# Splitting the first K tile's load of a decode-attention kernel into 16 and 112 partitions

## The chip, the cores and the metric

The kernel runs on one core of one Trainium2 chip. The metric is the device time of one execution in microseconds; the time of a kernel is the median of its runs.

## The reference

One decode step: grouped-query attention with 16 query heads on 8 KV heads over a cache of 65536 positions with 256 elements each, and a small gated feed-forward part, mixed by a sigmoid gate. Everything is bf16.

```python
q = (x @ wq)                                     # x: 1 x 448, wq: 448 x 4096 -> 16 heads x 256
scores = einsum("bhqd,bhkd->bhqk", q, k) * (256 ** -0.5)   # k, v: 8 heads x 65536 x 256, repeated twice
p = softmax(scores, axis=-1)
a = einsum("bhqk,bhkd->bhqd", p, v).reshape(1, 1, 4096) @ wo   # wo: 4096 x 448
gate, up = x @ W_gate, x @ W_up                  # 448 x 1792 each
b = (gate * (gate > 0) * up) @ W_down            # 1792 x 448
g = sigmoid((x * gate_w).sum(-1))
out = g * a + (1 - g) * b
```

K and V are 268 MB each, so nearly all bytes that the kernel reads are the two caches.

## The kernel before

**Tiles.** The K cache is read in 32 tiles, four for each of the 8 KV heads (`NTH = 4`, `NT = 32`). A tile is 16384 positions: 128 partitions with 128 positions each, 64 KB for a partition, 8 MB in all. `k_src(n)` gives the source of tile `n`, in which the 128 partitions' pieces follow one another in the cache. The V cache has 32 tiles of the same size. Three buffers of that size, `ring[0]` to `ring[2]`, hold what is on chip: K tiles go to 1 and 2 in turn, V tiles to 0 (the last head's V tiles to 1 and 2 as well). At the start, `ring[0]` holds the weights: wq (L626, and its last 64 rows L627), W_down (L675), then W_gate and W_up (L640, L642). At the end, wo is loaded in six pieces (L785).

**Order of transfers.** All large loads are issued from SP's program, in the order of the list `order`: K tile 0, wq, K tile 1, W_down, K tile 2, W_gate and W_up, then K and V tiles in turn. Each entry has a planned time `t`, which is only a key to sort by. `dma(engine, key, semaphore, function, dependences)` adds a transfer; `op` adds an instruction. `finish` sorts each engine's program by key. A transfer adds 16 to its semaphore when it has landed, and `finish` counts these, so that a dependence on a transfer becomes a wait for that count. `emit` writes out a program and puts the waits in front of each instruction; a wait for a count that the engine has already waited for is left out. `free(("k", n))` gives the work after which a buffer may be filled again; for K tiles 0 and 1 there is none. The two small loads, x and gate_w, are issued from ACT (L421, L422).

**What is done with a K tile.** DVE transposes it in place in four parts (L529, the operations `tr`), TensorE multiplies it with the query (L540, two halves `qk[n, 0]` and `qk[n, 1]`), DVE takes the maximum (L703) and ACT the exponential (L705). K tile 2 can be issued only when `qk[0, 1]` has read the buffer. For head 0 the query must be there first: TensorE projects it from wq (L501), ACT copies it (L630), DVE transposes it and spreads it into `xm` (L632, L513), ACT copies `xcur` (L634). DVE works through its program in order, and the four transposes of tile 0 stand ahead of L632. V tiles are multiplied by the probabilities on TensorE (L584) after a copy on ACT (L591).

**The start of SP's program.** The first operation of SP's program is written out ahead of the block in which the other engines' programs stand, and the rest in SP's part of the block, with one memory of the waits (`seen_sp`):

```python
        seen_sp = {}
        pl.emit("sp", progs["sp"][:1], nc.sync, seen_sp)
        with nc.Block() as block:
            @block.sync
            def _(e):
                pl.emit("sp", progs["sp"][1:], e, seen_sp)
```

Of the kernel before, what the change touches and what calls it, by code (L numbers as in the profile page):

```python
# [27 lines left out]
class _Plan:  # L28
# [8 lines left out]
    def op(self, eng, key, fn, deps=(), tag=None):  # L37
        eng, cls = {"pv": ("pe", "pv"), "dx": ("dv", "dx"), "ap": ("ac", "ap")}.get(eng, (eng, eng))
        o = _Op(eng, key, fn, deps, tag=tag, cls=cls)
        self.ops.append(o)  # L40
        return o

    def dma(self, eng, key, sem, fn, deps=()):
        if sem not in self.dsem:
            self.dsem[sem] = self.es.enter_context(self.nc.semaphore("d_" + sem))
        o = _Op(eng, key, fn, deps, dma=sem)
        self.ops.append(o)
        return o
# [212 lines left out]
def bass_gated_mix__gqa_block_cached__glu_gated_reglu__decode_kernel(  # L261
# [35 lines left out]
    with es:  # L297
# [3 lines left out]
        ring = [sb("ring%d" % i, [128, U * DH], BF) for i in range(NRING)]  # L301
# [68 lines left out]
        pl = _Plan(nc, es)  # L370
        op, dma = pl.op, pl.dma
# [23 lines left out]
        t = 3.0  # L395
# [10 lines left out]
        def place(kind, i):  # L406
            if kind == "k":
                return 1 + i % 2
            if kind == "v":
                return 1 + i % 2 if i >= NT - NTH else 0  # L410
            return {"vp": 2, "wo": 0}[kind]

        for kind, i, _ in order:
            if kind in ("k", "v") or (kind, i) in (("wo", 0), ("vp", 0)):
                r = place(kind, i)
# [101 lines left out]
        def k_src(n):  # L517
            h, t_ = divmod(n, NTH)
            return A_k_cache[0, h, t_ * TK:(t_ + 1) * TK, :].rearrange("(p u) d -> p (u d)", u=U)
# [7 lines left out]
        def f_trans(sl, w):  # L527
            v = ring[sl][:, w * 8192:(w + 1) * 8192].bitcast(U32)
            return lambda e: e.transpose(v, v)  # L529
# [34 lines left out]
        def free(key):  # L564
            out_ = []
            for f in freed[key]:
                out_.append(l_[f] if isinstance(f, str) else qk[f[1], 1] if f[0] == "k" else pv[f[1]])
            return out_
# [55 lines left out]
        for kind, i, t in sorted(issue, key=lambda q: q[0] != "wq"):  # L624
# [51 lines left out]
            elif kind == "k":  # L676
                n = i
                h, t_ = divmod(n, NTH)
                sl = slot["k", n]
                kd = dma("sp", t, "r%d" % sl, lambda e, n=n, sl=sl: e.dma_start(ring[sl][:], k_src(n)), free(("k", n)))  # L680
                tk = max(tL["k", n], last.get("free", 0))
                tr = [op("dv", tk + 4.5 * w, f_trans(sl, w), [kd]) for w in range(4)]
                if n > 1:
                    tr[1].deps.append(aexp[n - 2])
                if t_ == 0:
# [82 lines left out]
            elif kind in ("v", "vp"):  # L768
                if kind == "v":
                    n, lo, hi = i, 0, U  # L770
                    sl = slot["v", n]
                    dep = dma("sp", t, "r%d" % sl, lambda e, sl=sl, n=n: e.dma_start(ring[sl][:], v_src(n)), free(("v", n)))
                else:
                    n, (lo, hi) = NT - 1, PIECES[i]
                    sl = slot["vp", 0]
# [7 lines left out]
            elif kind == "wo":  # L783
                lo, hi = WO[i]
# [19 lines left out]
        progs = pl.finish()  # L804

        seen_sp = {}
        pl.emit("sp", progs["sp"][:1], nc.sync, seen_sp)
        with nc.Block() as block:

            @block.sync  # L810
            def _(e):
                pl.emit("sp", progs["sp"][1:], e, seen_sp)

            @block.tensor
            def _(e):
                prog = progs["pe"]
                at = lambda o: prog.index(o)
                seen = {}
                k0 = [at(pv[NTH * (h - 1)] if h else qk[0, 0]) for h in range(H)]
                km = [at(pv[NTH * (h - 1) + 2] if h else qk[2, 0]) for h in range(H)]  # L820
                kc = [at(last["h3", h]) for h in range(H)]
                t0, t1, t2 = at(pv[NT - NTH]), at(pv[NT - 2]), at(pv[NT - 1]) + 1
                pl.emit("pe", prog[:k0[0]], e, seen)
                inner, outer = {}, {}
                for h in range(H):
                    inner[h, 0], inner[h, 1] = prog[k0[h]:km[h]], prog[km[h]:kc[h]]
                    outer[(h,)] = prog[kc[h]:k0[h + 1] if h < H - 1 else t0]
                pl.emit_nest("pe", e, inner, outer, seen, {("pv", a, 0) for a in range(2)} )
                pl.emit_loop("pe", e, {(0,): prog[t0:t1], (1,): prog[t1:t2]}, seen)
                pl.emit("pe", prog[t2:], e, seen)  # L830

            @block.vector
            def _(e):
                pl.emit_heads("dv", progs["dv"], e, [first["dv", h] for h in range(1, H)] + [last["ocp", H - 1]], 1)

            @block.scalar
            def _(e):
                pl.emit_heads("ac", progs["ac"], e, [first["ac", h] for h in range(1, H)] + [pc[NT - NTH]], 1)

            @block.gpsimd  # L840
            def _(e):
                pl.emit("gp", progs["gp"], e)
# [33 lines left out]
```

## Time and profile before

| | before |
|---|---|
| time, median of 3 runs | 1275.85 us (1275.74 to 1276.02) |
| profiled execution: span from first to last instruction | 1274.3 us |
| bytes read | 549.03 MB, 431 GB/s over the span |
| busy share: PE, DVE, ACT, POOL | 29%, 49%, 6%, 0% |
| issue of K tile 0 on SP | at 0.72 us |
| first transpose of K tile 0 on DVE | at 22.81 us |
| first matmul of the q projection | at 31.49 us |
| issue of K tile 2 on SP | at 50.70 us |
| output's transfer issued | at 1273.11 us |

The profile shows one execution. Its own whole time is not listed apart from its span; the runs' median is 1.55 us above the span, which stands for what lies ahead of the first and behind the last instruction. In the lines of the profile, PE is TensorE's matmul, PEld its weight load, DVE VectorE, ACT ScalarE, POOL GpSimd, and an engine's name with a q is its queue of instructions that issue transfers. `L529` is line 529 of the kernel.

### The profile page before, as it was taken

The numbers are of one execution on the slowest core, as the hardware profiler recorded it, in microseconds if no ns is written. First come the engines' busy times: TensorE is split into PE (matmuls) and PEld (weight loads), VectorE is DVE, ScalarE is ACT, GpSimd is POOL, SyncE is SP. The second block draws the span as 40 slices with busy tenths as digits, with TensorE's granted clock in tenths as the row PEclk, the third lists the DMA queues.
The fourth block names the chain that finished last, engine by engine and source line by source line (L and its number), as shares of the span: only waits on it lengthen the run. The fifth ranks groups of instructions, "written<-read, shape, count | busy, mean of one in ns | idle before, by whom it ended". The sixth has DMA issues, their size and how long they took to land.

```text
span 1274.3 us, 10240 instructions
## 1 busy us (share of the span) xinstructions
PE 365.9 (29%) x4497; PEld 151.4 (12%) x4505; DVE 630.1 (49%) x309; ACT 78.0 (6%) x163; POOL 4.6 (0%) x23
## 2 busy tenths in 40 slices
PE   0534321133320332312233222323302332112525
PEld 0101110011110111101111110111100111001201
DVE  4777655553455633557433565335654355553300
ACT  0001100010000100001000010000000010000100
POOL 1000000000000000000000000000000000000000
PEclk9766665666655666656666656666566666566667
DMA  9999999999999999999999999999999999999998
GB/s 411 430 436 432 426 430 434 432 443 432 430 432 432 434 442 430 430 434 430 438 438 430 430 434 430 440 438 428 430 434 430 444 434 428 430 436 430 442 421 369
DMA packets 11389, 549.13 MB, mean 431 GB/s; under 512 B 1267, under 2 KB 1654, under 8 KB 2294
## 3 DMA queue, kind: packets, MB, share of 16 engines
q1 hardware_dynamic: 11378, 549.03, 99.7%
q8 instruction: 4, 0.07, 0.0%
q14 instruction: 3, 0.02, 0.0%
q10 hardware_dynamic: 4, 0.00, 0.0%
HBM read 549.03 MB, written 0.00 MB: 431 GB/s over the span
## 4 chain that ended last, share of the span: by engine, by line
DMA 81%; PE 16%; DVE 2%; ACT 1%; issue 1%; SPq 0%; ACTq 0%
DMA ring<-in_A_v_cache_dram 74%; PE O L584 13%; DMA ring<-in_A_wo_dram 3%; DMA ring<-in_A_wq_dram 2%; DMA ring<-in_A_k_cache_dram 2%; DVE ring L529 1%; PE ST L540 1%; ACT pcur L591 1%; PE O L501 1%; PE A_ps L551 0%; SPq L785 0%; SPq L776 0%; PE O L653 0%; DVE ring L660 0%; PE A_ps L653 0%
## 5 line engine op out<-in xcount | busy, mean ns | idle before, releaser
L529 DVE STREAM_TRANSPOSE ring<-ring 128x4096 uint32<-128x4096 uint32 x128 | 557.6, 4413 | 196.9 <-DMA ring<-in_A_k_cache_dram 196.9
L584 PE MATMUL O<-ring,pcur 128*4 128x512 bf16 x2048 | 187.3, 545 | 790.4 <-ACT pcur L591 781.9
L703 DVE TENSOR_REDUCE nmb<-ST 128x1 f32<-128x512 f32 x32 | 22.1, 692 | 345.9 <-PE ST L540 345.9
L584 PEld LDWEIGHTS O<-ring,pcur 128*4 128x4 bf16 x2048 | 59.3, 111 | 914.8 <-ACT pcur L591 794.6
L540 PE MATMUL ST<-ring,xcur 128*16 128x512 bf16 x2048 | 136.7, 420 | 44.3 <-DVE ring L529 43.7
L540 PEld LDWEIGHTS ST<-ring,xcur 128*16 128x16 bf16 x2048 | 62.4, 92 | 112.1 <-DVE ring L529 48.6
L705 ACT ACTIVATE P_sb<-ST,nmb 128x512 bf16<-128x512 f32 x32 | 44.6, 1392 | 368.3 <-DVE nmb L703 368.3
L591 ACT COPY pcur<-ptp 128x256 bf16<-128x256 bf16 x32 | 13.2, 415 | 732.6 <-DMA ring<-in_A_v_cache_dram 732.6
L607 DVE TENSOR_SCALAR o_sb<-O,rcm 128x256 bf16<-128x256 f32 x8 | 3.8, 479 | 61.1 <-PE O L584 61.1
L730 DVE TENSOR_TENSOR P_sb<-P_sb,hs 128x1024 bf16<-128x1024 bf16 x16 | 18.9, 1222 | 8.1 <-ACT hs L724 8.1
L735 PE MATMUL PT<-identb,P_sb 128*128 128x128 bf16 x128 | 14.5, 282 | 17.6 <-DVE P_sb L730 17.3
L501 PE MATMUL O<-ring,P_sb 128*128 128x512 bf16 x28 | 8.5, 477 | 17.3 <-DMA ring<-in_A_wq_dram 17.3
L735 PEld LDWEIGHTS PT<-identb,P_sb 128*128 128x128 bf16 x128 | 10.7, 127 | 19.9 <-DVE P_sb L730 19.9
L744 ACT COPY ptp<-PT 128x256 bf16<-128x256 bf16 x32 | 10.3, 375 | 23.0 <-PE PT L735 23.0
L705 ACT ACTIVATION_READ_ACCUMULATOR P_sb<-ST,nmb 128x1 f32 x32 | 8.3, 258 | 0.0
L501 PEld LDWEIGHTS O<-ring,P_sb 128*128 128x128 bf16 x28 | 3.2, 117 | 22.2 <-issue 20.5
L551 PE MATMUL A_ps<-ring,attnA 128*1 128x224 bf16 x64 | 5.3, 322 | 1.1 <-DMA ring<-in_A_wo_dram 1.0
L719 PE MATMUL M_ps<-identf,hs 128*2 128x128 f32 x8 | 2.3, 283 | 10.0 <-DVE hs L717 10.0
L756 DVE RECIPROCAL rc<-M_ps 128x2 f32<-128x2 f32 x8 | 1.4, 171 | 7.5 <-PE M_ps L755 7.5
L755 PE MATMUL M_ps<-hs,ones_f 128*128 128x2 f32 x16 | 4.5, 352 | 0.0
L722 PE MATMUL M_ps<-mx,nselT 2*128 2x1 f32 x16 | 3.2, 268 | 3.0 <-DVE mx L721 3.0
L755 PEld LDWEIGHTS M_ps<-hs,ones_f 128*128 128x128 f32 x16 | 4.0, 311 | 0.0
(93 smaller groups left out, 68.6 us busy)
## 6 DMA issues: line engine op xcount, KB each, us to landing
ring<-in_A_v_cache_dram SPq DMA_DIRECT2D x1, 4096.0 KB, 22.1
ring<-in_A_wq_dram SPq DMA_DIRECT2D x1, 3072.0 KB, 28.9
ring<-in_A_v_cache_dram SPq DMA_DIRECT2D x1, 3072.0 KB, 28.8
ring<-in_B_W_down_dram SPq DMA_DIRECT2D x1, 1568.0 KB, 53.0
ring<-in_B_W_gate_dram SPq DMA_DIRECT2D x1, 1344.0 KB, 26.3
ring<-in_B_W_up_dram SPq DMA_DIRECT2D x1, 1344.0 KB, 29.2
ring<-in_A_wo_dram SPq DMA_DIRECT2D x1, 1232.0 KB, 33.0
ring<-in_A_v_cache_dram SPq DMA_DIRECT2D x1, 1024.0 KB, 30.7
```

Source lines behind the costliest of these rows:

```text
L501: ins = e.matmul(QN_ps, xw3[:, kt, 31 - m:159 - m], rhs, start=(kt == 0 and m == 0), stop=(kt == R3 and m == J // 4 - 1))
L529: return lambda e: e.transpose(v, v)
L540: ins = e.matmul(bank[32 * w:32 * w + 16, :], xcur[:, x0:x0 + 16], ktv[sl][:, u0:u0 + 16, c, :, r_], start=(b == 0 and c == 0 and r_ == 0) ...
L551: ins = e.matmul(A_ps[32 * g:32 * g + 1, 0:D2], lhsT, rhs[:, g * D2:(g + 1) * D2], start=start, stop=stop, skip_group_check=True, tile_pos ...
L584: ins = e.matmul(OP[32 * g:32 * g + 4, :], pcur[a % 2][:, 4 * k:4 * k + 4], ring[sl][:, k * 512:(k + 1) * 512], start=False, stop=False, s ...
L591: pc[n] = op("ap", max(tp - 5, last["tev", h] - 0.5), lambda e: e.copy(pcur[a % 2][:].rearrange("p (k i) -> p k i", i=4), ptp[:].rearrange ...
L703: smax[n] = op("dv", sx, lambda e, n=n, t_=t_: e.tensor_reduce(NM[:, t_:t_ + 1], ST[n % 2][:], AX.X, ALU.max, negate=True), [qk[n, 1], las ...
L705: aexp[n] = op("ac", sx + 1, lambda e, n=n, t_=t_: e.activation(P_sb[:, t_:2048:4], ST[n % 2][:], ACTF.Exp, bias=NM[:, t_:t_ + 1], scale=1 ...
L730: rsc = op("dv", tt, lambda e, pb=pb: e.tensor_tensor(pb, pb, X[:, 12:16].unsqueeze(1).to_broadcast([128, 256, 4]), ALU.mult), [h7, aexp[n]])
L735: ins = e.transpose(PT[rd][:, s * 128:(s + 1) * 128], P_sb[:, (rd * 8 + s) * 128:(rd * 8 + s + 1) * 128], identb[:, :])
L744: ins = e.copy(dst, src)
L755: l3 = mop("pe", T + 19, lambda e: e.matmul(LS_ps, ones_f[:, :], X[:, 6:8], start=True, stop=True), [l2, c_one], tag="l3")
```

## The change

K tile 0 is loaded by two transfers in place of one. The first takes partitions 0 to 15, that is 16 pieces of 64 KB, and has a semaphore of its own, `k0`. The second takes partitions 16 to 127, 112 pieces, on the semaphore that the one transfer had. All other K tiles stay one transfer. The transposes of tile 0 depend on both. Both transfers are written out ahead of the block, so that the split of SP's program moves from one operation to two.

```diff
                 sl = slot["k", n]
-                kd = dma("sp", t, "r%d" % sl, lambda e, n=n, sl=sl: e.dma_start(ring[sl][:], k_src(n)), free(("k", n)))
+                cuts = [0, 16, 128] if n == 0 else [0, 128]
+                kd = [dma("sp", t + 0.001 * j, "k0" if n == j == 0 else "r%d" % sl, lambda e, n=n, sl=sl, lo=lo, hi=hi: e.dma_start(
+                    ring[sl][lo:hi, :], k_src(n)[lo:hi, :]), free(("k", n))) for j, (lo, hi) in enumerate(zip(cuts, cuts[1:]))]
                 tk = max(tL["k", n], last.get("free", 0))
-                tr = [op("dv", tk + 4.5 * w, f_trans(sl, w), [kd]) for w in range(4)]
+                tr = [op("dv", tk + 4.5 * w, f_trans(sl, w), kd) for w in range(4)]
...
         seen_sp = {}
-        pl.emit("sp", progs["sp"][:1], nc.sync, seen_sp)
+        pl.emit("sp", progs["sp"][:2], nc.sync, seen_sp)
         with nc.Block() as block:
 
             @block.sync
             def _(e):
-                pl.emit("sp", progs["sp"][1:], e, seen_sp)
+                pl.emit("sp", progs["sp"][2:], e, seen_sp)
```

## The prediction

> **What bounds the kernel now.** I read the page's DMA lines first, then the chain of work that ended last, then the first microseconds in narrow windows, because the change touches nothing later than the first transfer.
>
> The page (queue line: packets, MB, share of 16 engines' span):
>
> ```profile
> span 1274.3 us, 10240 instructions
> DMA  9999999999999999999999999999999999999998
> ...
> q1 hardware_dynamic: 11378, 549.03, 99.7%
> ...
> DMA 81%; PE 16%; DVE 2%; ACT 1%; issue 1%; SPq 0%; ACTq 0%
> ```
>
> 549 MB come in over one queue, and its packets fill 99.7% of what 16 DMA engines have in 1274.3 us. Idle per engine is 0.3% of that, 3.8 us. The windows (last two columns: DMA share, put where a packet starts, so that it can pass 1; GB/s) show where that idle time lies:
>
> ```profile
> 0.00:1.50 1.50, 0.00 (x0) 0.00 (x0) 0.68 (x5) 0.00 (x0) 0.79 (x6) 1.00 0.00 0
> ...
> 1.75:2.00 0.25, 0.00 (x0) 0.00 (x0) 0.25 (x1) 0.00 (x0) 0.23 (x1) 1.00 6.44 2097
> 2.00:2.25 0.25, 0.00 (x0) 0.00 (x0) 0.20 (x3) 0.00 (x0) 0.25 (x1) 1.00 5.30 1835
> 2.25:2.50 0.25, 0.00 (x0) 0.00 (x0) 0.14 (x3) 0.00 (x0) 0.17 (x2) 1.00 0.00 0
> 2.50:2.75 0.25, 0.00 (x0) 0.00 (x0) 0.19 (x2) 0.00 (x0) 0.12 (x1) 1.00 0.70 262
> 2.75:4.50 1.75, 0.00 (x0) 0.00 (x0) 1.51 (x4) 0.00 (x0) 1.28 (x7) 1.00 0.00 0
> 4.50:5.00 0.50, 0.00 (x0) 0.00 (x0) 0.47 (x3) 0.00 (x0) 0.35 (x2) 1.00 1.51 655
> 5.00:6.00 1.00, 0.27 (x5) 0.21 (x5) 0.52 (x5) 0.00 (x0) 0.75 (x4) 1.00 1.66 721
> ```
> ```profile
> 60.00:1200.00 1140.00, 318.10 (x4049) 133.45 (x4057) 591.34 (x252) 71.01 (x148) 0.00 (x0) 0.62 1.00 433
> ...
> 1272.00:1274.30 2.30, 0.56 (x10) 0.09 (x4) 0.38 (x1) 0.34 (x1) 0.00 (x0) 1.00 0.00 0
> ```
>
> About 1.75 us pass before the first packet and some 2 us after the last; together that is the whole 3.8. Between them the engines never run dry (share 1.00, 433 GB/s). So a microsecond that all engines lose at the start is not caught up, and one that is won there is kept, if the work between the transfers moves with them. The chain of waits says that it does:
>
> ```profile
> 1.66 29.70 DMA ring<-in_A_wq_dram
> 31.35 0.14 issue
> 31.49 8.51 PE O L501 x28
> ...
> 50.70 24.64 DMA ring<-in_A_k_cache_dram
> 75.37 17.43 DVE ring L529 x4
> ...
> 104.18 36.90 DMA ring<-in_A_v_cache_dram
> ...
> 1236.40 35.84 DMA ring<-in_A_wo_dram
> ```
>
> The first thing that counts is the landing of wq, which stands behind K tile 0 in the queue. Then the q projection, the scores of tile 0, the issue of K tile 2 at 50.70, and from there load after load up to wo. Each of these hangs on a transfer.
>
> The windows also give the packets. Bytes over time count them: 2097 GB/s in 0.25 us is 524 KB, eight packets of 64 KB (one row of a K tile); 1835 makes seven, 262 one: sixteen first packets, which start over 0.5 to 1 us. They take 6.44 x 0.25 x 16 / 8 = 3.2 us each. Nothing starts from 2.75 to 4.50. In the 5.00 to 6.00 row eleven packets start (721 KB), with 1.66 x 16 / 11 = 2.41 us each. That is 27.2 GB/s for one engine, and sixteen times that is the 433 of the long row. A K tile is 128 rows, eight for each engine: 8 x 2.41 = 19.3 us.
>
> **The change, part by part.**
>
> One more instruction on SP. The issues now, and the first work that waits for K tile 0:
>
> ```profile
> 0.72 0.42 SPq L680 DMA_DIRECT2D ring<-in_A_k_cache_dram  x1
> ...
> 1.20 0.41 SPq L626 DMA_DIRECT2D ring<-in_A_wq_dram  x1
> ...
> 2.12 0.54 SPq L680 DMA_DIRECT2D ring<-in_A_k_cache_dram  x1
> 2.71 0.53 SPq L675 DMA_DIRECT2D ring<-in_B_W_down_dram  x1
> ...
> 4.92 0.18 DVE L478 COPY scr<-P_sb 1x64 bf16<-1x64 bf16 x1
> ...
> 10.15 0.61 DVE L464 TENSOR_TENSOR ptp<-P_sb,scr 1x448 f32<-1x448 bf16 x1 [3.93 <-DMA scr<-in_gate_w_dram]
> ...
> 22.81 17.42 DVE L529 STREAM_TRANSPOSE ring<-ring 128x4096 uint32<-128x4096 uint32 x4 [8.20 <-DMA ring<-in_A_k_cache_dram]
> ```
>
> The second half of K tile 0 takes the place at 1.20, and wq, its last rows, K tile 1 and W_down each go out 0.48 us later. Their packets stand behind K tile 0's, until about 22 us; that covers the delay, which would cost 0.48 without it. Nothing: 0.
>
> The second half must be in the queue before the first runs out. It is issued at 1.2, and today an issue at 0.72 has its last engine going by 2.75, 2.0 us later; so by 3.2. The first packets end at 4.5 to 5.2 today. Covered by over a microsecond: 0.
>
> The first DVE transpose waits for two semaphores in place of one. Behind it on DVE stand the other transposes and the q path's; all need the same tile. The wait ends with the later landing, so it costs nothing of its own.
>
> Small loads on ACT's queue (x, gate_w) share the engines. If K's first packets start sooner or last longer, x may come one packet later than its 4.92 and gate_w later than 10.15. The first is needed at 31.49 by L501 and the second at 40.0, after L501's 8.51 us: over 20 us of cover, 0.
>
> The start. A transfer of 16 packets may get all engines going sooner than one of 128. The bound on a gain: the sixteenth engine starts up to 1.0 us after the first (1.75 to 2.75), and the slowest engine sets the end, so at most 1.0. The bound on the other side is 0. I take 0.3, since fifteen of sixteen start within 0.5 us.
>
> The rows written at once. This is the term that decides, and no row of the trace shows it: every large transfer there spans 128 partitions, with each engine on its own rows. The new transfer has sixteen engines write sixteen neighbouring partitions at once. The trace's 27.2 GB/s may be the pace of an engine or of the path that it writes to in SBUF; 16 x 27.2 = 433 fits either. If it is the path's, with 128 partitions spread evenly over sixteen paths, then eight rows belong to one path, and sixteen neighbours lie on sixteen paths at best and on two at worst. The first packets then take 2.41 us (sixteen paths), 4.8 (eight), 9.6 (four) or 19.3 (two), in place of 2.41. I take four paths, about the middle of these on a scale of ratios: 9.6 - 2.4 = 7.2 us lost on every engine. Ends: 0 and 16.9.
>
> [...]
>
> The other 112 rows. Seven for each engine, 7 x 2.41 = 16.9 us if no two meet. If they are dealt in runs of seven, the engines no longer stand on paths of their own. Sixteen engines on sixteen paths without order leave (15/16)^16 = 36% of the paths empty, so 16.9 / 0.64 = 26.2 us, or 9.3 lost. Engines that meet fall out of step, and then meet less: I take half, 4.7. Ends: 0 and 9.3.
>
> The sum: 7.2 + 4.7 - 0.3 = 11.6 us. The profiled execution shows its span of 1274.3; the median of the three runs, 1275.85, is 1.55 more, which I take as what lies around the span. 1274.3 + 11.6 + 1.55 = 1287.5 us.
>
> **The rivals.**
>
> Forecast (paths are shared): for it, the steady 2.41 us of all packets in 128-row transfers, with nothing to be seen of engines meeting, as if rows were dealt so that they don't. With the two ends of its terms (eight paths and half of the taken loss afterwards: 2.4 + 2.3 - 0.3 = 4.4; four paths and the full 9.3: 7.2 + 9.3 - 0.3 = 16.2) it gives 1280 to 1292. Two paths, or engines that stay in each other's way in the next transfer, would give more. 56%.
>
> An engine's own pace is the limit (no price, small gain): sixteen rows in 2.4 us, then seven in 16.9, the same eight packets per engine as before. What is left is the earlier start, 0 to 1.0 us: 1274.9 to 1275.9. This ends on the other side, not slower. It decides if the first sixteen packets of the new trace take about 3.2 us as before, under 5 at any rate. For it: a packet's 2.41 us fits an engine's limit as well as a path's. It would also come out so if the sixteen rows went to a few engines in such an order that each has eight in all. 34%, with 2% more for a gain beyond 0.2% (2.55 us), which would take away more than the 1.75 us before the first packet.
>
> The 112 rows are dealt one by one (engine e takes rows e, e + 16 and so on): then sixteen neighbours are written at once eight times over, 8 x 7.2 = 58 us lost, 1333 us. Against it: it needs four shared paths and that order both. 8%.
>
> That the change does less than it says, with the tile still as one packet stream, would be the second case too: the transfers differ in their rows alone.
>
> **How the numbers follow.** The likeliest case gives 1287.5, its own range 1280 to 1292. The range over cases takes in the second case from 1274.9 and reaches 3 us past the likeliest's own for what its last sentence names; the 8% case and tails are left out. A measurement of this kernel can tell about 0.2% (2.55 us) from no change: slower 56 + 8 = 64%, within 34%, faster 2%.
>
> **What would show it right or wrong.** The windows from 1.5 to 12 us: in my forecast sixteen packets start by 2.5 us and hardly any before 9, and their share times 16 gives near 10 us for each; in the second case new packets start from 4.5 on, as today. The first L529 transpose then begins near 34 (22.81 + 11.6), not 22.5, and everything behind it, such as the issue of K tile 2 (50.70) and the last wo load, is later by the same amount; share and GB/s from 60 us on stay as they are. If L529 moves and the end doesn't, the claim that a loss is never caught up is wrong. If the first packets take 10 us but the rest of the tile runs in 16.9, the second term is wrong, and the sum is 1282.8.

## The result, and the profile after

The kernel with the split takes 1296.53 us (median of five runs, 1295.96 to 1297.21) against 1275.87 before: 20.66 us longer, ratio 1.0162, 95% interval 1.015 to 1.0174. Its profiled execution has a span of 1294.5 us, 20.2 more than 1274.3. The forecast was 1287.5, with 1295.0 as the upper end.

From the page, first the GB/s line of the kernel before (forty equal slices of the span), then the lines of the kernel after:

```profile
GB/s 411 430 436 432 426 430 434 432 443 432 430 432 432 434 442 430 430 434 430 438 438 430 430 434 430 440 438 428 430 434 430 444 434 428 430 436 430 442 421 369
```
```profile
span 1294.5 us, 10250 instructions
DMA  9999999999999999999999999999999999999998
GB/s 219 352 418 441 441 427 435 437 427 440 429 431 439 429 433 437 427 439 429 431 439 429 435 435 429 437 429 433 439 427 437 433 429 437 431 435 435 429 431 366
...
q1 hardware_dynamic: 11394, 549.03, 99.7%
```

The bytes are the same and the share of busy time of the DMA engines is the same 99.7%. Of these lines only GB/s tells what happened: 219 and 352 in the first two slices, where before every slice but the last stands above 400. An engine whose packet crawls counts as busy.

The windows of the kernel after (the last two columns are DMA share, put where a packet starts, and GB/s):

```profile
1.50:2.75 1.25, 0.00 (x0) 0.00 (x0) 0.98 (x9) 0.00 (x0) 0.96 (x4) 1.00 6.78 840
2.75:9.00 6.25, 0.27 (x5) 0.21 (x5) 2.67 (x10) 0.00 (x0) 2.85 (x14) 1.00 0.00 0
9.00:11.50 2.50, 0.00 (x0) 0.00 (x0) 0.00 (x0) 0.00 (x0) 0.00 (x0) 1.00 2.26 420
11.50:15.50 4.00, 0.00 (x0) 0.00 (x0) 1.22 (x2) 1.37 (x2) 0.00 (x0) 1.00 0.00 0
15.50:17.00 1.50, 0.58 (x2) 0.50 (x2) 0.59 (x4) 0.11 (x1) 0.00 (x0) 1.00 3.10 699
17.00:20.00 3.00, 0.00 (x0) 0.00 (x0) 0.23 (x1) 0.00 (x0) 0.00 (x0) 1.00 0.00 0
20.00:22.00 2.00, 0.00 (x0) 0.00 (x0) 0.00 (x0) 0.00 (x0) 0.00 (x0) 1.00 1.59 524
...
23.00:24.50 1.50, 0.00 (x0) 0.00 (x0) 0.00 (x0) 0.00 (x0) 0.00 (x0) 1.00 2.19 612
24.50:27.00 2.50, 0.00 (x0) 0.00 (x0) 0.00 (x0) 0.00 (x0) 0.00 (x0) 1.00 0.18 52
27.00:28.50 1.50, 0.00 (x0) 0.00 (x0) 0.00 (x0) 0.00 (x0) 0.00 (x0) 1.00 2.38 568
28.50:30.00 1.50, 0.00 (x0) 0.00 (x0) 0.00 (x0) 0.00 (x0) 0.00 (x0) 1.00 0.56 131
31.00:33.00 2.00, 0.00 (x0) 0.00 (x0) 0.00 (x0) 0.00 (x0) 0.00 (x0) 1.00 1.88 426
33.00:35.00 2.00, 0.00 (x0) 0.00 (x0) 0.00 (x0) 0.00 (x0) 0.00 (x0) 1.00 0.43 98
35.00:39.00 4.00, 0.00 (x0) 0.00 (x0) 0.00 (x0) 0.00 (x0) 0.00 (x0) 1.00 1.13 262
```

The packets come in eight waves of sixteen packets, one for each row of the tile that an engine is dealt. In the first line 840 GB/s over 1.25 us is 1.05 MB, sixteen packets; share times length is the mean time of one, since sixteen engines share sixteen packets: 6.78 x 1.25 = 8.5 us. The next wave starts between 9.0 and 11.5. The waves of the 112 rows take 5.65 (2.26 x 2.5), 4.65, 3.18, 3.74 (2.19 x 1.5 + 0.18 x 2.5), 4.41, 4.62 and 4.52 us: 30.8 together, where seven rows at 2.42 are 16.9. Here 2.42 us is the time of a packet before, once it runs. No wave is at the pace of before, and they are not alike: the third and fourth of the 112 are the cheap ones.

The timeline of the kernel after (start, duration, engine and line):

```profile
44.59 17.43 DVE L529 STREAM_TRANSPOSE ring<-ring 128x4096 uint32<-128x4096 uint32 x4 [27.34 <-DMA ring<-in_A_k_cache_dram]
...
53.22 7.57 PE L501 MATMUL O<-ring,P_sb 128*128 128x512 bf16 x28 [36.43 <-DMA ring<-in_A_wq_dram]
...
71.28 0.33 SPq L681 DMA_DIRECT2D ring<-in_A_k_cache_dram  x1
```
```profile
100.00:1200.00 1100.00, 300.39 (x3855) 123.97 (x3855) 569.39 (x242) 67.35 (x141) 0.00 (x0) 0.62 1.00 434
```

The first transpose starts at 44.59 (22.81 before, +21.8), the projection at 53.22 (+21.7), the issue of K tile 2 at 71.28 (+20.6). From 100 us on the engines run as they did, at 434 GB/s. All of the loss stands before 45 us, and 20.2 us of it are there at the end. The 21.8 us of the first transpose is more than that, because the transpose waits for the last packet: the packets of the last wave start anywhere from 35 to 39 us, where before fifteen of the sixteen start from 19 to 20.

### The profile page after: what moved, and what is told of

Its sections match the earlier page's. It is cut to its first block, busy times and chain, and to the rows that moved or that the text cites. A ratio compares the mean times of both kernels' runs of the same rounds, so it can differ in the third digit from the quotient of the medians.

```text
span 1294.5 us, 10250 instructions
## 1 busy us (share of the span) xinstructions
PE 363.9 (28%) x4505; PEld 148.1 (11%) x4505; DVE 630.0 (49%) x309; ACT 78.0 (6%) x163; POOL 4.6 (0%) x23
## 3 DMA queue, kind: packets, MB, share of 16 engines
q1 hardware_dynamic: 11394, 549.03, 99.7%
## 4 chain that ended last, share of the span: by engine, by line
DMA 78%; PE 15%; another core or an unknown queue 3%; DVE 2%; ACT 1%; issue 1%; SPq 0%; ACTq 0%
DMA ring<-in_A_v_cache_dram 73%; PE O L584 13%; DMA ring<-in_A_wo_dram 3%; DMA ring<-in_A_k_cache_dram 2%; DVE ring L529 1%; PE ST L540 1%; ACT pcur L591 1%; DMA scr<-in_gate_w_dram 1%; PE O L501 1%; PE A_ps L551 0%; SPq L787 0%; SPq L778 0%; ACT L466 0%; PE O L653 0%
## 5 line engine op out<-in xcount | busy, mean ns | idle before, releaser
L584 PE MATMUL O<-ring,pcur 128*4 128x512 bf16 x2048 | 183.5, 536 | 790.4 <-ACT pcur L591 782.2
L571 PE MATMUL O<-zer,identb 128*128 128x512 bf16 x8 | 4.7, 587 | 0.0
```

The source lines that it names most:

```text
L571: last["zo", h] = op("pv", key, lambda e: e.matmul(OP[:], identb[:, :], zer[:, 0:1].to_broadcast([128, 512]), start=True, stop=True, skip_ ...
L584: ins = e.matmul(OP[32 * g:32 * g + 4, :], pcur[a % 2][:, 4 * k:4 * k + 4], ring[sl][:, k * 512:(k + 1) * 512], start=False, stop=False, s ...
```

## The experiments

The theory going in is the forecast's: some partitions are written through a path that they share, and engines that write through the same path at the same time share its speed. Which partitions those are, the runs have to tell. The rivals: a split costs in itself; rows of the cache that lie side by side are slow to read; the late wq and not the queue makes the end late. Each time below stands beside the kernel before on the same chip, 1275.9 to 1276.0 us. The edits are given in short, not as the code has them.

**The same first megabyte, cut by columns.**

```diff
-cuts 0, 16, 128 on partitions of tile 0
+columns 0:4096 of all 128 partitions, then columns 4096:32768
```

> K tile 0 again comes in two transfers, the first of 1 MB, but cut by columns: 8 KB of each of the 128 partitions, then 56 KB of each. [...] Rival (a split of the first tile costs in itself, by its second issue, its semaphore or its order among the engines): about the 20 us of the change again, 1290 to 1297.

Measured 1275.8 us, ratio 0.9999 (0.999 to 1.0009). Two transfers, a second semaphore and 1 MB in the first cost nothing, so the split in itself isn't it. Nor does it gain anything.

**Eight transfers of 16 partitions, neighbours and then every eighth.**

```diff
-cuts 0, 16, 128
+e2: partitions 0:16, 16:32, ..., 112:128      e3: 0:128:8, 1:128:8, ..., 7:128:8
```

> K tile 0 in eight transfers of 16 neighbouring partitions. Shared paths: every one of them is on four paths, 8 x 4 x 2.42 = 77.4 us for the tile in place of 19.3, so 1334 us; with the 8.4 us that the first sixteen packets of the change took, of which about 0.8 belongs to the start, 8 x 7.6 = 61 and 1318 at the lowest. Rival (the loss comes from the seven-row deal of the 112 and the first 16 rows lose only their start): at most 5 us, 1276 to 1281.

> The same eight transfers of 16 rows, but each takes every eighth partition (0, 8, ..., 120; then 1, 9, ...). [...] If eight neighbours share a path, all sixteen are apart and it is 1276. Rival (sixteen-row transfers are slow whichever rows they take): the same time as eight transfers of neighbours, 1318 to 1334.

Measured 1330.99 us (ratio 1.0431, 1.0414 to 1.0449) for neighbours and 1297.28 (1.0168, 1.0151 to 1.0185) for every eighth. The windows of the two, first of neighbours:

```profile
9.00:11.50 2.50, 0.00 (x0) 0.00 (x0) 0.00 (x0) 0.00 (x0) 0.00 (x0) 1.00 3.72 420
```
```profile
4.40:9.00 4.60, 0.27 (x5) 0.21 (x5) 1.85 (x8) 0.00 (x0) 1.64 (x8) 1.00 1.11 228
```

Both lines hold sixteen packets (1.05 MB): 3.72 x 2.5 = 9.3 us each for neighbours, 1.11 x 4.6 = 5.1 for every eighth. Same bytes, same count of transfers, other partitions: 55.1 us lost or 21.4. So it depends on the partitions; that some sixteen cost next to nothing, the loads ahead below show (1278.63 us with 32:96:4, of which 2.4 are the pace of before for 1 MB more). 9.3 is 3.8 times the 2.42 of a packet alone, 5.1 is 2.1 times; if it is a shared path, that is four writers on each in the one case and two in the other. On that reading, as an estimate, a path with four writers gives 4 x 65536 B in 9.3 us, 28 GB/s, and one with two 25.7. Sixteen neighbours together run at 113 GB/s (1.05 MB in 9.3 us) once going, against 433 (1.05 MB in 2.42 us) in the kernel before.

**The 112 rows written out as seven transfers.**

```diff
-cuts 0, 16, 128
+partitions 0:16, then 16:128:7, 17:128:7, ..., 22:128:7
```

> First the 16 partitions 0 to 15 as in the change, then the other 112 as seven transfers with step 7 (16, 23, ..., 121; then 17, 24, ... and so on), which is the order in which sixteen engines would write if each was dealt a run of seven neighbours. If the 112 are dealt so, packets go as in the change (about 5.5, 4.6, 3.0, 3.6, 4.4, 4.6 and 4.4 us) and the time is 1296.5 within 2. If they are dealt in another way, the time differs: by two engines on a path at most and no mutual holding up it would be 1284 to 1290.

Measured 1296.55 us, against 1296.53 for the change. Its windows:

```profile
9.00:11.50 2.50, 0.00 (x0) 0.00 (x0) 0.00 (x0) 0.00 (x0) 0.00 (x0) 1.00 2.18 419
...
18.00:22.00 4.00, 0.00 (x0) 0.00 (x0) 0.00 (x0) 0.00 (x0) 0.00 (x0) 1.00 0.83 262
```

2.18 x 2.5 = 5.45 us for the first wave, 5.65 in the change, and 0.83 x 4 = 3.3 for the third, 3.18 in the change. The first four, read in the same way, take 5.5, 4.8, 3.3 and 3.8 us, each within 0.2 us of the change's. So the one transfer of 112 partitions behaves as if each engine is dealt a run of seven neighbours: engine e writes 16 + 7e, 17 + 7e and so on. That was assumed in the forecast and is now shown by time and waves alike.

**Halves, and every fourth.**

```diff
-cuts 0, 16, 128
+e5: partitions 0:64, 64:128      e12: 0:128:4, 1:128:4, 2:128:4, 3:128:4
```

> K tile 0 in two transfers of 64 partitions, 0 to 63 and 64 to 127. [...] If a half is as good as the whole as long as every engine gets a run of neighbours: 1276.

> K tile 0 in four transfers of 32 partitions, each every fourth partition (0, 4, ..., 124, then 1, 5, ...). [...] If it counts which rows are written at the same time, and each engine is dealt a run of two rows (partitions 8e and 8e + 4): eight paths at a time, two engines on each, 5.1 us a packet and 1297 us.

Measured 1297.26 us for the halves (ratio 1.0167, 1.015 to 1.0184) and 1276.33 for every fourth (1.0003, 0.9993 to 1.0013). The windows of the halves, then of every fourth:

```profile
4.40:9.00 4.60, 0.27 (x5) 0.21 (x5) 1.24 (x7) 0.00 (x0) 1.64 (x8) 1.00 1.11 228
```
```profile
4.40:9.00 4.60, 0.27 (x5) 0.21 (x5) 2.21 (x9) 0.00 (x0) 1.64 (x8) 1.00 1.06 456
```

In a half sixteen packets take 5.1 us each. With every fourth partition 32 packets start in the same stretch (456 GB/s x 4.6 us = 2.1 MB) and take 1.06 x 4.6 x 16 / 32 = 2.44: full speed. A transfer of 64 whole neighbours is slow and one of 32 spread ones is not. My deal for the 32 (runs of two, and so every eighth partition at once, at 5.1 us a packet) is wrong: the rows are dealt so that no packet is slowed. How, this run doesn't say. The whole tile of 128 can't be dealt in runs either: runs of eight would write every eighth partition at once, as the eight transfers did at 5.1 us a packet, and the whole tile's packets take 2.42.

**The split on K tile 1.**

```diff
-cuts 0, 16, 128 if n == 0
+cuts 0, 16, 128 if n == 1
```

> The split of the change, 16 and 112 partitions, but of K tile 1; tile 0 is one transfer. Tile 1 stands behind wq in the queue, and its first use comes half a tile's time after its landing before. If a loss in the queue is never caught up: 1296 us, with wq's landing and the first matmul of the projection at 31.4 us as before, and K tile 2's landing about 20 us later. Rival (the loss of the change came by the late wq and the late query, and the slack behind tile 1 hides part of it): 1276 to 1290.

Measured 1296.69 us (ratio 1.0164, 1.0147 to 1.0181). Its timeline:

```profile
31.88 7.52 PE L501 MATMUL O<-ring,P_sb 128*128 128x512 bf16 x28 [17.53 <-DMA ring<-in_A_wq_dram]
49.10 0.35 SPq L681 DMA_DIRECT2D ring<-in_A_k_cache_dram  x1
...
73.04 17.42 DVE L529 STREAM_TRANSPOSE ring<-ring 128x4096 uint32<-128x4096 uint32 x4 [23.24 <-DMA ring<-in_A_k_cache_dram]
```

The projection starts only 0.4 us later than before, and K tile 2 is issued at 49.10, even earlier than 50.70. The last line is the transposes of tile 1, which began at 52.11 before. The end is 20.8 us late. So it is the queue that carries the loss, wherever in it the slow tile stands, and not the late query.

**Writing or reading.** In these kernels tile 0 is one transfer, and 16 rows of tile 1 are loaded once more than needed ahead of it.

```diff
+if n == 0: dma k0: ring[2][DST, :] <- k_src(1)[SRC, :]      (tile 1's own transfer waits for it)
 e7: DST 0:16, SRC 0:16     e8: DST 0:16, SRC 0:128:8     e9: DST 0:128:8, SRC 0:16
```

> K tile 0 comes in one transfer as before. Ahead of it 16 rows of K tile 1 are loaded once more than needed, to partitions 0 to 15 of tile 1's buffer, from rows 0 to 15 of tile 1 in the cache; tile 1's own transfer waits for them. Both theories (shared write paths; neighbouring rows of the cache are slow to read): first sixteen packets of 8.4 us, of which 0.8 belongs to the start, so 1275.9 + 7.6 = 1283.5 us. If the 112-row transfer's deal had been needed for the loss: 2.4 us for the bytes alone, 1278.3.

> The same load ahead to partitions 0 to 15, but read from every eighth row of tile 1 (its contents are overwritten by tile 1's own load). Shared write paths: only the destination counts, so as with neighbouring rows, 8.4 us for the first packets and 1283.5 us. Rival (the reading side: sixteen neighbouring 64 KB rows of the cache meet in the memory): as every eighth row in the eight transfers, near 4.9 us and 1280 us.

> The same load ahead, read from rows 0 to 15 and written to every eighth partition. Shared write paths: eight paths, 4.9 us for the first packets, 1275.9 + 4.1 = 1280 us. Rival (the reading side): as from neighbouring rows, 8.4 us and 1283.5 us.

Measured 1285.11, 1285.11 and 1281.08 us. The first windows of the three, in this order:

```profile
1.50:2.80 1.30, 0.00 (x0) 0.00 (x0) 1.03 (x9) 0.00 (x0) 1.01 (x5) 1.00 6.50 807
```
```profile
1.50:2.80 1.30, 0.00 (x0) 0.00 (x0) 1.03 (x9) 0.00 (x0) 1.01 (x5) 1.00 6.63 807
```
```profile
1.50:2.80 1.30, 0.00 (x0) 0.00 (x0) 1.03 (x9) 0.00 (x0) 1.01 (x5) 1.00 2.90 606
2.80:4.00 1.20, 0.00 (x0) 0.00 (x0) 0.98 (x3) 0.00 (x0) 0.90 (x5) 1.00 0.96 218
```

Packets of 8.5 and 8.6 us to partitions 0 to 15, wherever they are read, and of 4.9 (2.90 x 1.3 + 0.96 x 1.2) to every eighth, read from neighbours. The destination decides and the source does not. The reading side is out. All three times are 1 to 1.6 us above what I expected: the wave behind is slower too. Its sixteen packets, the first of tile 0, take 3.7, 3.8 and 2.9 us on the mean in place of 2.4.

**How many must meet.** The same load ahead, to six other sets of sixteen partitions, each read from the rows with the same numbers. Of the sets with step four, 28:92:4 is 32:96:4 with row 28 in place of 92, and 24:88:4 is 28:92:4 with row 24 in place of 88.

```diff
 e14: 32:96:4     e13: 11:117:7     e15: 28:92:4     e10: 18:124:7
 e16: 24:88:4     e11: 16:128:7 (the first wave of the 112)
```

> [...] If sixteen-row transfers cost something however they lie: 1280 or more.

> [...]

> [...]

> The load ahead goes to partitions 18, 25, ..., 123, read from the same rows. [...]

> [...]

> [...]

| destination | packets that start from 4.0 to 5.8 us | time, us | ratio, 95% interval |
|---|---|---|---|
| 32:96:4 | 16 | 1278.63 | 1.0021 (1.0012 to 1.0031) |
| 11:117:7 | 13 | 1279.73 | 1.003 (1.002 to 1.0041) |
| 28:92:4 | 14 | 1280.15 | 1.0034 (1.0021 to 1.0046) |
| 18:124:7 | 12 | 1281.01 | 1.004 (1.0026 to 1.0054) |
| 24:88:4 | 0 | 1280.92 | 1.0039 (1.0025 to 1.0053) |
| 16:128:7 | 0 | 1281.8 | 1.0045 (1.0029 to 1.0062) |

The times differ by little and don't decide alone. The 1278.63 of 32:96:4 lies below the 1280 or more of a price for sixteen rows however they lie. The windows say more, above all the one from 4.0 to 5.8 us, in which an engine that wasn't slowed starts its second packet. First 32:96:4, then 11:117:7:

```profile
1.50:2.80 1.30, 0.00 (x0) 0.00 (x0) 1.03 (x9) 0.00 (x0) 1.01 (x5) 1.00 2.20 757
2.80:4.00 1.20, 0.00 (x0) 0.00 (x0) 0.98 (x3) 0.00 (x0) 0.90 (x5) 1.00 0.13 55
4.00:5.80 1.80, 0.27 (x5) 0.21 (x5) 1.25 (x6) 0.00 (x0) 1.26 (x7) 1.00 1.36 583
```
```profile
4.00:5.80 1.80, 0.27 (x5) 0.22 (x5) 1.26 (x6) 0.00 (x0) 1.26 (x7) 1.00 1.28 474
```

Then 28:92:4, 18:124:7 and 24:88:4:

```profile
1.50:2.80 1.30, 0.00 (x0) 0.00 (x0) 1.03 (x9) 0.00 (x0) 1.01 (x5) 1.00 2.13 706
2.80:4.00 1.20, 0.00 (x0) 0.00 (x0) 0.98 (x3) 0.00 (x0) 0.90 (x5) 1.00 0.37 109
4.00:5.80 1.80, 0.27 (x5) 0.21 (x5) 1.26 (x6) 0.00 (x0) 1.26 (x7) 1.00 1.52 510
```
```profile
4.00:5.80 1.80, 0.27 (x5) 0.22 (x5) 1.25 (x6) 0.00 (x0) 1.28 (x7) 1.00 1.39 437
```
```profile
1.50:2.80 1.30, 0.00 (x0) 0.00 (x0) 1.03 (x9) 0.00 (x0) 1.01 (x5) 1.00 3.06 706
2.80:4.00 1.20, 0.00 (x0) 0.00 (x0) 0.98 (x3) 0.00 (x0) 0.90 (x5) 1.00 0.41 109
4.00:5.80 1.80, 0.27 (x5) 0.21 (x5) 1.26 (x6) 0.00 (x0) 1.26 (x7) 1.00 0.00 0
```

With 32:96:4, 583 GB/s x 1.8 us = 1.05 MB start in the last line: all sixteen packets. With 28:92:4, 510 GB/s x 1.8 us = 0.92 MB, fourteen packets. The other two start theirs between 5.8 and 8 us (60 GB/s x 2.2 us = 0.13 MB). With that one row exchanged two engines are late, which fits two rows in each other's way, row 28 and one of the other fifteen. (Which engines these are, the windows don't say.) The first packets take 3.21 us on the mean (2.13 x 1.3 + 0.37 x 1.2), against 3.02 with 32:96:4; two at the 5.1 of every eighth partition and fourteen at 3.02 would make 3.28. But the second packets of the fourteen take 3.13 us (1.52 x 1.8 x 16 / 14), where with 32:96:4 they take 2.45: the fourteen are slowed too, one packet later. With one more row exchanged, in 24:88:4, none starts: all sixteen are slow, 4.47 us on the mean (3.06 x 1.3 + 0.41 x 1.2). Had row 24 made two more engines late and no others, four packets at 5.1 and twelve at 3.02 would make 3.5. The 4.47 is not far from the 4.9 of the load to every eighth partition. The load to 16:128:7 shows the same empty line and 4.73 us. That is what I had not allowed for.

With step 7 the picture is less sharp: thirteen start there with 11:117:7 (474 GB/s) and twelve with 18:124:7 (437). The first packets of 11:117:7 take 3.24 us, 0.2 more than those of 32:96:4, and its time is 1.1 us longer. Whether that comes from the order of the rows or from rows in each other's way is not shown. It is little beside the 1.5 us that the first packets take longer with 24:88:4.

## Why the prediction was right or wrong

The sign, the place and most of the mechanism were right: the sixteen neighbours that slow one another, the deal in sevens, the wait of everything for the queue. The size was wrong, 20.66 us against 11.6, and by one term, with the idea behind it of how engines meet.

- *Issue, semaphores, small loads: 0.* Right. SP's further issues are later, gate_w's first use went from 10.15 to 12.78, and the column cut shows that none of it costs.
- *The start: 0.3 gained.* Wrong, and small: the sixteen engines get going between 1.5 and 2.75 us as before. The transfer of sixteen packets starts no sooner than the one of 128: eight of the sixteen start only from 2.50 to 2.75, where before fifteen had started by 2.25.
- *The first sixteen rows: 7.2 lost.* The time of four paths was nearly right, a packet of 8.5 us beside the 9.6 (and 9.3 once going, in the eight transfers); that there are paths, and how many, no run shows. But four was taken as the middle of what is possible, so that the sum had the right number there is luck. The term was too large, since the first packets of before already took 3.1 us (their share times time, over sixteen packets) and not 2.4: 8.5 - 3.1 = 5.4.
- *The 112 rows: 4.7 lost, at most 9.3.* This is the step that failed. The run of seven was right. Taking half, because "engines that meet fall out of step, and then meet less", was not, and even the end of the term assumed that an engine without company keeps its pace. The rows of the first wave, loaded alone (16:128:7), hold up all sixteen engines at once, at 4.73 us a packet, and so does 24:88:4, at 4.47, which differs from 28:92:4 in one row. In the change the engines don't fall so far out of step that the waves mix: between one wave and the next there is always a stretch in which no packet starts, such as 11.5 to 15.5 and 17 to 20. That the next rows meet again because of it is argued, not tested by itself. Measured: 30.8 - 16.9 = 13.9, against the 4.7 taken and the 9.3 at most. The rows by themselves don't give all of it: the 5.65 of the first wave is above the 4.73 of the same rows alone. The prediction names engines that stay in each other's way as what would give more, but it gives that no time.
- *The sum.* 5.4 + 13.9 = 19.3 of the 20.2 us of span. Most of the rest is in the first packets of wq behind the tile, which I didn't forecast:

```profile
40.00:43.00 3.00, 0.00 (x0) 0.00 (x0) 0.00 (x0) 0.00 (x0) 0.00 (x0) 1.00 0.71 213
```

These carry 213 GB/s x 3 us = 0.64 MB and keep an engine 0.71 x 3 = 2.1 us, where the pace of before (1.05 MB in 2.42 us) makes 1.5. With these 0.7 us it is 20.0 of the 20.2.
- *Never caught up.* Right: 21.7 us at the projection, 20.6 at K tile 2, 20.2 at the end, and nearly the same (20.8) with the slow tile further back in the queue.
- *The rivals.* The engine's own pace (34%) is out: packets of one size take 2.4, 5.1 or 9.3 us by their destination. The one-by-one deal (8%) is out by the waves, though its price, 58 us, is near the 55.1 of the eight transfers that do just that.
- *A slip.* 16 x 27.2 is 435, not the 433 that the prediction gives; nothing hangs on it.

What stays open: why 24:88:4 holds up all sixteen engines at once, and 28:92:4 two of them, with the fourteen slowed only in the packets behind; how much the order of the rows adds by itself; and what the engines share. The runs show only which of these sets of partitions are slow to write together.

## What to carry to other kernels

Cut a load by columns and leave its 128 partitions whole: the same 1 MB ahead costs nothing by columns (1275.8 us) and 20.66 us by partitions. Four transfers of every fourth partition cost nothing either (1276.33). If partitions must be cut, what counts is which rows the sixteen engines write at the same moment, so that a remainder such as 112, dealt in sevens, can cost more than the piece cut off (13.9 us against 5.4). And a DMA share of 99.7% doesn't say that the queue runs well: read the GB/s beside it.

## What the runs showed of the hardware that was not expected

A load to 24:88:4 slows all sixteen engines to 4.5 us a packet at once, where with 28:92:4, which differs in one row, fourteen start their second packet on time and lose only then (3.13 us in place of 2.45). Sixteen packets together move 433 GB/s in the kernel before (2.42 us each), 206 to every eighth partition (5.1 us) and 113 to sixteen neighbours (9.3 us). Thirty-two partitions in steps of four load at 2.44 us a packet, as fast as all 128.
